# Attention and mixture of experts on one core: transposes as two 64-row halves, eight blocks to two PSUM banks, with six buffers for q and k

## The chip, the cores and the metric

The kernel runs on one core of one Trainium2 chip. The metric is the device time in microseconds of one execution, the median over several runs.

## The reference, cut to what matters

```python
def _attn_ref(q, k, v):                       # each (8, 8, 576, 64): batch, heads, sequence, head dim
    chunk = 64                                # 9 chunks of 64 positions, each attends to itself alone
    scores = (1 / np.sqrt(D)) * np.matmul(q_c, k_c.transpose(0, 1, 2, 4, 3))
    scores = scores - np.max(scores, axis=-1, keepdims=True)
    attn = np.exp(scores)
    attn = attn / (np.sum(attn, axis=-1, keepdims=True) + 1e-09)
    return np.matmul(attn, v_c).reshape(B, H, S, D)

def _moe_ref(x, w_gate, w_local, w1, w2):     # x: (8, 576, 512), 8 experts, F = 1024
    # each token takes the expert of its largest logit, or the one of the token before it,
    # as a local gate says; p is the softmax of the logits
    h = np.maximum(x[b, s] @ w1[e], 0.0)
    out[b, s] = p[e] * (h @ w2[e])
```

All of it is float32.

## The kernel before, in words

The 4608 tokens are 18 attention tiles of 256 tokens (four chunks of 64; tiles 4 and 13 are "mixed", they gather the ninth chunks of four batches). A tile goes through these steps, each a list of small functions ("atoms"):

- `load_qk` and `load_v` (lines 137 and 153) issue the DMAs of q, k and v on SP's queue. q and k have three buffers each, v has three (`vbuf`, the first in the raw tiles of w2).
- `pair_heads` (line 166, token `pr` or `p0` to `p3`) copies q and k into `qr` and `kr`, so that two heads lie side by side: 8 blocks of 128 rows by 128 columns each.
- `qk_transposes` (line 203, token `tq`) turns them over on TensorE: 8 blocks of q, 8 of k. `trans4` (line 186) takes four blocks into one PSUM bank (tile `tr`, pool `ps_tr` with three banks) and then has the bank copied out to `qT` or `kT`.
- `scores` (line 220, token `s`): 64 small matmuls 64x64 on the four quadrants of the array, then the largest of each row (`top`), the subtraction (`down`) and the exponential (`exp`).
- `p_transposes` (line 258, `tp`): 8 blocks of the probabilities, copied out to `pT`.
- `values` (line 267, `va`): two groups of 32 small matmuls, with `norm` behind each, into `xs`.
- `x_transposes` (line 304, `tx`): 8 blocks of `xs`, copied out to `xT`.
- `router` (line 312, `ra`): the logits (`lg`, 8 matmuls with 32 stationary columns each), two transposes, and the DMA of `xs` with its logits to `x_d` in DRAM.

In the trace TensorE's transposes all have line 192 and ScalarE's copies line 182, so they are told apart by their tiles. A transpose takes its block as the stationary operand and the identity as the moving one.

The order of the work on TensorE, VectorE, ScalarE and GpSimd is written out by hand in strings of tokens (`PAR`, line 47; `play`, line 523, walks through them): `"start"` brings in tiles 0 to 2, `"steady"` is one iteration of the loop on line 866 (i from 1 to 15, in which tile i+1 has its scores, tile i its probabilities turned, tile i-1 its values, tile i-2 its `xs` turned and routed, tile i+2 its q and k turned, tile i+3 paired, and q, k of tile i+5 and v of tile i+2 are loaded), and `"drain"` ends the attention and interleaves it with the routing and the first expert tiles. From i = 10 on, "hooks" (`h0` to `h3`) put the routing of the first half of the tokens between the tokens of the iteration, mostly on VectorE. From i = 8 to 15 each iteration also splits half a w1 tile. Loads are issued by SP in the order of the program and wait there for their buffer.

After the drain come the expert layers (lines 961 to 1222), which the change doesn't touch. Their w2 tiles `w2h` and `w2l` are first written in the drain (`w2_split`, line 882).

Of the kernel before, what the change touches and what calls it, by code (L numbers as in the profile page):

```python
# [8 lines left out]
F32 = mybir.dt.float32  # L9
F32R = mybir.dt.float32r  # L10
# [10 lines left out]
B, H, S, D = 8, 8, 576, 64  # L21
E, F = 8, 1024
C = H * D
N = B * S
P = 128
# [4 lines left out]
HT = P // 2  # L30
# [15 lines left out]

PAR = {
    "start": (
        "p0*4 t0a*4 t0a t0b*4 t0b t0c*4 t0c t0d*4 t0d p1*4 q3 t1a*4 t1a s0*8 t1b*4 t1b s0*2 t1c*4 t1c "
        "q4 t1d*4 t1d p2*4 s0*4 s1*8 t2a*4 t2a t2b*4 t2b s1*2 o0*4 o0 o0*4 o0 s1 t2c*4 t2c t2d*4 t2d s1*3 q5 v2 p3*4 io "  # L50
    ),
    "drain": (
# [13 lines left out]
    "t0": "VAVA",  # L66
    "t1": "AAAA",
    "t2": "AVAA",
    "steady": "lq va*4 va s*8 s h0 tx*8 tq*8 s h1 va*4 lv ra*2 va h2 tq*8 ra*2 tp*8 s pr*4 h3 ",
    "hooks": [43, 43, 45, 46, 47, 48, 49, 49, 51, 51, 52, 53, 54, 55, 55, 56, 57, 58, 59, 61, 61, 62],  # L70
}

# [2 lines left out]
def tile_attention_then_moe(ctx: ExitStack, tc, q, k, v, wg, wl, w1, w2, out):  # L75
    nc = tc.nc

    cpool = ctx.enter_context(tc.tile_pool(name="cpool", bufs=1))
    wpool = ctx.enter_context(tc.tile_pool(name="wpool", bufs=1))
# [7 lines left out]
    ident = cpool.tile([P, P], F32, name="ident")  # L87
# [2 lines left out]

    w1h = [wpool.tile([P, F], F32R, name=f"w1h{c}") for c in range(4)]
    w1l = [wpool.tile([P, F], F32R, name=f"w1l{c}") for c in range(4)]
    w2h = [wpool.tile([P, 2, C], F32R, name=f"w2h{c}") for c in range(4)]
    w2l = [wpool.tile([P, 2, C], F32R, name=f"w2l{c}") for c in range(4)]
    raw1 = [wpool.tile([P, F], F32, name=f"raw1_{c}") for c in range(4)]
    raw2 = [wpool.tile([P, 2, C], F32, name=f"raw2_{c}") for c in range(4)]

# [3 lines left out]
    def load_w2(e, c):  # L101
        nc.sync.dma_start(raw2[c], w2[e, 256 * c:256 * c + 256, :].rearrange("(f p) d -> p f d", p=P))
# [16 lines left out]
    ps_o = ctx.enter_context(tc.tile_pool(name="ps_o", bufs=1, space=PSUM))  # L119
    ps_l = ctx.enter_context(tc.tile_pool(name="ps_l", bufs=1, space=PSUM))  # L120

    vbuf = [[raw2[c].rearrange("p f (h d) -> p (f h) d", d=2 * D) for c in (2, 3)]]
    for i in range(2):
        vt = pa1.tile([P, VS], F32, name=f"v{i}")[:, 0:2 * H * DW].rearrange("p (c h d) -> p c h d", c=2, d=DW)
        vbuf.append([vt[:, c] for c in range(2)])

    def place(i):
        ph, j = divmod(i, 9)
# [5 lines left out]
    def mixed_rows(i):  # L134
        return i % 9 == LEFT

    def load_qk(i):
        qt = pe2.tile([P, 8 * 2 * D], F32, name="qt", tag="qt", bufs=3)
        kt = pe2.tile([P, 8 * 2 * D], F32, name="kt", tag="kt", bufs=3)
# [12 lines left out]

    def load_v(i):
        vt = vbuf[i % 3]
# [25 lines left out]
    def evac(eng, dst, src):  # L180
        if eng is nc.scalar:
            eng.copy(dst, src)
        else:
            eng.tensor_copy(dst, src)

    def trans4(src_of, evacs, fine=False):
        box = {}

        def one(n):
            if n == 0:  # L190
                box["ps"] = ps_tr.tile([P, 4, P], F32, name="tr")
            nc.tensor.transpose(box["ps"][:, n], src_of(n), ident)
            if n == 3 and not fine:
                for m in range(len(evacs)):
                    out(m)

        def out(m):
            eng, dst, sl = evacs[m]
            evac(eng, dst, sl(box["ps"]))

        return [lambda n=n: one(n) for n in range(4)] + [lambda m=m: out(m) for m in range(len(evacs)) if fine]

    def qk_transposes(i, hd, qT, kT, engs=None):
        atoms = []
        fine, engs = engs is not None, engs or QK_ENG
        for n, t in enumerate((qT, kT)):
            for x in range(2):
                if mixed_rows(i):
                    src = hd[n].rearrange("p (r h) j d -> p r h (j d)", r=2)[:, x]
                    dst = t.rearrange("a h (c p r) -> a r h c p", c=4, r=2)[:, x]  # L210
                    how = lambda ps: ps.rearrange("a h (p c) -> a h c p", c=4)
                else:
                    src = hd[n].rearrange("p (l x) j d -> p x l (j d)", x=2)[:, x]
                    dst = t.rearrange("a g (p l x) -> a x g p l", l=4, x=2)[:, x]
                    how = lambda ps: ps.rearrange("a l (p g) -> a g p l", g=4)
                atoms += trans4(lambda m, src=src: src[:, m], [(engs[2 * n + x], dst, how)], fine)
        return atoms


# [36 lines left out]
                      lambda: down(1), lambda: exp(4, 8)]  # L256

    def p_transposes(pr, pT, fine=False):
        atoms = []
        for g in range(2):  # L260
            atoms += trans4(
                lambda n, g=g: pr[:, 4 * g + n].rearrange("p c k -> p (c k)"),
                [(nc.scalar, pT[:, 4 * g:4 * g + 4], lambda ps: ps)], fine)
        return atoms


    def values(pT, vt, xs, fine=False):
        box = {}

        def group(j, h):  # L270
            if h == 0:
                box["o"] = ps_o.tile([P, 2, 512], F32, name="o")
            o = box["o"]
            for cp in range(2):
                for cc in range(2):
                    nc.tensor.matmul(
                        o[64 * cp:64 * cp + 64, cc, DV * h:DV * h + D + 1],
                        pT[64 * cc:64 * cc + 64, 4 * j + h, 64 * cp:64 * cp + 64],
                        vt[cp][64 * cc:64 * cc + 64, 4 * j + h, 0:D + 1],
                        start=True, stop=True,  # L280
                    )
# [14 lines left out]

        out = []
        for j in range(2):
            out += [lambda j=j, h=h: group(j, h) for h in range(4)]
            if fine:  # L300
                out.append(lambda j=j: norm(j))
        return out

    def x_transposes(xs, xT, fine=False):
        atoms = []
        for cc in range(2):
            atoms += trans4(
                lambda n, cc=cc: xs[:, cc, P * n:P * n + P],
                [(nc.scalar, xT[:, :, P * cc:P * cc + P], lambda ps: ps)], fine)
        return atoms  # L310

    def router(i, xT, xs, fine=False):
        lg = ps_l.tile([P, 2, 256], F32, name="lg")
# [174 lines left out]
    qk, hd, vts, qkT, prs, pTs, xss, xTs = ({} for _ in range(8))  # L488
# [11 lines left out]
        return scores(*qkT.pop(i), prs[i], fine)  # L500

    def a_tp(i, fine=False):
        pTs[i] = pa2.tile([P, H, P], F32, name="pT")
        return p_transposes(prs.pop(i), pTs[i], fine)

    rows = []
# [85 lines left out]
    with tc.manual_schedule(engines=MAN | {ET.Pool}):  # L592
# [10 lines left out]
        def tq(i, g):  # L603
# [283 lines left out]

    for c in range(2):
        load_w2(0, c)
    n = NS - 1  # L890
    sa = a_sa(n, True)
    run(sa[0:8])
# [351 lines left out]
```

## Time and profile before

| | |
|---|---|
| median of 3 runs | 650.43 us (645.71 to 650.65) |
| the profiled execution | 652.38 us |
| its span in the profile | 650.5 us, 1.9 us of that time lie around it |
| TensorE matmuls, weight loads | 94%, 79% of the span |
| VectorE, ScalarE, GpSimd | 58%, 39%, 23% |
| granted TensorE clock, mean | 0.991 of full |

A span is read from the first instruction to the last on the slowest core. PE is TensorE's matmul row, PEld its weight loads, DVE VectorE, ACT ScalarE, POOL GpSimd, SP SyncE. A matmul's record covers its whole way through the array, so consecutive records overlap: what one costs in a stream is the step from start to start. An instruction of matrix multiplication in float32 shows as two matmuls in scores, values and logits, a transpose as one.

### The profile page before, as it was taken

What the parts mean: (1) busy time and instruction counts of PE and PEld (TensorE: products, weight loads), DVE (VectorE), ACT (ScalarE), POOL (GpSimd) and SP (SyncE); (2) the same over time, 40 slices, a digit from 0 to 9 for tenths busy, and PEclk for the clock granted to TensorE, in tenths of its full rate; (3) what the DMA queues carried; (4) which work ended last, traced back from release to release, by engine and by line L of the source; (5) the groups of instructions that cost most, each with busy time, mean ns of one, the idle gap of its engine ahead of it and who ended that gap; (6) DMA issues with size and microseconds to landing.
All of it is one profiled execution on the core that took longest, in us unless ns stands there. A gap on an engine that the chain in (4) does not pass through costs nothing. (4 is left out here: it accounts for less than half of the span.)

```text
span 650.5 us, 17406 instructions
## 1 busy us (share of the span) xinstructions
PE 613.0 (94%) x5904; PEld 516.4 (79%) x5904; DVE 377.2 (58%) x983; ACT 256.5 (39%) x469; POOL 147.5 (23%) x217
## 2 busy tenths in 40 slices
PE   5889998999999999999999999999998999999995
PEld 4677777776778788788998996789887998788883
DVE  2666677986785667575334555753468533377231
ACT  4666675774421162532112343422454311343120
POOL 3623343570050302021021021031021222011101
PEclk9999998999999999999999999999998999999998
DMA  8799989998540155155021164442075511054201
GB/s 258 207 266 285 267 250 320 292 267 295 164 148 19 52 165 181 31 179 182 20 69 53 54 209 129 147 176 69 20 261 199 189 53 55 32 181 142 74 21 37
DMA packets 78360, 97.89 MB, mean 150 GB/s; under 512 B 42672, under 2 KB 46768, under 8 KB 78192
## 3 DMA queue, kind: packets, MB, share of 16 engines
q1 hardware_dynamic: 71744, 75.30, 37.1%
q0 software_dynamic: 6160, 19.99, 9.3%
q8 instruction: 86, 1.41, 0.9%
q14 instruction: 82, 0.67, 0.3%
q10 hardware_dynamic: 288, 0.52, 0.2%
HBM read 76.62 MB, written 19.69 MB: 148 GB/s over the span
## 5 line engine op out<-in xcount | busy, mean ns | idle before, releaser
L801 POOL DMA_INDIRECT out<-ysb,sidx x38 | 40.9, 1076 | 364.3 <-DVEq L997 163.3
L740 PE MATMUL y<-w2h,hq 128*128 128x512 f32 x368 | 119.8, 396 | 1.1 <-ACTq L1019 1.0
L1032 PEld LDWEIGHTS tr<-xp,w1h 128*128 128x128 f32 x704 | 87.8, 192 | 4.0 <-ACT w2h L981 1.1
L1032 PE MATMUL tr<-xp,w1h 128*128 128x256 f32 x704 | 90.2, 284 | 0.7 <-ACTq L997 0.4
L740 PEld LDWEIGHTS y<-w2h,hq 128*128 128x128 f32 x368 | 69.6, 189 | 16.7 <-issue 2.1
L740 PE MATMUL y<-w2l,hq 128*128 128x512 f32 x184 | 72.5, 394 | 2.6 <-DVE w2l L987 1.5
L1040 ACT ACTIVATE hq<-tr 128x256 fp32r<-128x256 f32 x68 | 25.3, 384 | 107.1 <-PE tr L1032 70.7
L740 PE MATMUL y<-w2h,hp 128*128 128x512 f32 x192 | 63.1, 396 | 0.4 <-ACT hp L687 0.3
L719 PE MATMUL h<-w1h,xp 128*128 128x512 f32 x208 | 60.8, 398 | 0.0
L1041 DVE SCALAR_TENSOR_TENSOR hq<-tr,hq 128x256 fp32r<-128x256 f32 x68 | 28.1, 423 | 38.1 <-ACT hq L1040 38.0
L1032 PE MATMUL tr<-xp,w1l 128*128 128x256 f32 x352 | 47.6, 283 | 0.0
L1032 PEld LDWEIGHTS tr<-xp,w1l 128*128 128x128 f32 x352 | 44.6, 192 | 0.0
L719 PEld LDWEIGHTS h<-w1h,xp 128*128 128x128 f32 x208 | 37.9, 189 | 7.6 <-ACTq L997 0.4
L740 PEld LDWEIGHTS y<-w2l,hq 128*128 128x128 f32 x184 | 34.9, 190 | 10.4 <-DVE w2l L987 2.4
L691 POOL DMA_INDIRECT xg<-x_d,gidx x36 | 38.3, 1063 | 19.6 <-issue 12.5
L740 PEld LDWEIGHTS y<-w2h,hp 128*128 128x128 f32 x192 | 36.0, 188 | 8.2 <-DVE hp L688 0.6
L786 ACT ACTIVATE hsb<-h 128x512 f32<-128x512 f32 x26 | 14.1, 596 | 65.8 <-PE h L719 56.4
L1061 DVE TENSOR_SCALAR ysb<-y,ppr 128x512 f32<-128x512 f32 x32 | 24.0, 750 | 26.9 <-PE y L740 23.8
L987 DVE TENSOR_TENSOR w1l<-raw,w1h 128x1024 fp32r<-128x1024 f32 x28 | 32.4, 1220 | 12.1 <-ACT w1h L981 10.6
L740 PE MATMUL y<-w2l,hp 128*128 128x512 f32 x96 | 37.6, 392 | 0.5 <-DVE w2l L987 0.5
L987 DVE TENSOR_TENSOR w2l<-raw,w2h 128x1024 fp32r<-128x1024 f32 x28 | 32.8, 1221 | 5.2 <-ACT w2h L981 3.2
L981 ACT CAST w2h<-raw 128x1024 fp32r<-128x1024 f32 x28 | 28.1, 1047 | 14.8 <-PE y L740 6.2
(229 smaller groups left out, 1062.1 us busy)
## 6 DMA issues: line engine op xcount, KB each, us to landing
raw<-in_moe_w SPq DMA_DIRECT2D x72, 512.0 KB, 5.1
x_d<-xs SPq DMA_DIRECT2D x16, 528.0 KB, 6.1
qt<-in_q SPq DMA_DIRECT2D x32, 256.0 KB, 5.0
kt<-in_k SPq DMA_DIRECT2D x30, 256.0 KB, 5.0
v<-in_v SPq DMA_DIRECT2D x20, 256.0 KB, 5.3
raw<-in_v SPq DMA_DIRECT2D x12, 256.0 KB, 5.2
x_d<-xs SPq DMA_DIRECT2D x4, 264.0 KB, 4.9
qt<-in_q SPq DMA_DIRECT2D x8, 128.0 KB, 3.8
```

Source lines behind the costliest of these rows:

```text
L691: nc.gpsimd.indirect_dma_start(out=dst, out_offset=None, in_=src, in_offset=bass.IndirectOffsetOnAxis(ap=gidx[t].bitcast(U32), axis=0))
L719: nc.tensor.matmul(hs[:, j], xs[a][:, c], W1[w][c][:, 512 * j:512 * j + 512], start=(c == 0 and n == 0), stop=(c == 3 and n == 2))
L740: nc.tensor.matmul(y, h_of(t, f // 4)[a][:, f % 4], W2[w][c][:, f % 2, :], start=(f == 0 and n == 0), stop=(f == 7 and n == 2))
L786: nc.scalar.activation(hsb[:, 512 * j:512 * j + 512], hs[:, j], AF.Relu)
L801: nc.gpsimd.indirect_dma_start(out=out, out_offset=bass.IndirectOffsetOnAxis(ap=sidx[t].bitcast(U32), axis=0), in_=ysb, in_offset=None, bo ...
L981: nc.scalar.copy(hi[c], raw[c])
L987: V.tensor_tensor(lo[c], raw[c], hi[c].bitcast(F32), ALU.subtract)
L1032: nc.tensor.matmul(hb[:, 256 * n:256 * n + 256], W1[w][c][:, P * (f + n):P * (f + n) + P], XP[:, x, c].rearrange("p s t -> p (s t)"), star ...
L1040: nc.scalar.activation(hi, ps, AF.Relu)
L1041: V.scalar_tensor_tensor(lo, ps, 0.0, hi.bitcast(F32), ALU.max, ALU.subtract)
L1061: V.tensor_scalar(ysb, y, pr, None, ALU.mult)
```

## The change

`trans8` takes the place of `trans4`. It turns each 128x128 block by two transposes: rows 0 to 63 of the block with the upper left quarter of the identity into columns of one PSUM bank, rows 64 to 127 with the lower right quarter into another bank. Eight blocks fill the two banks (8 times 64 columns each), and one copy empties each bank. The number of copies, and the elements of each, stay as they were. A group takes two of the three `tr` banks at once. `pT` gets the layout `[P, 2, H, 64]`, and `values` reads it so.

The buffers for q and k become six: three own ones and three in the tiles of w2 (`lent`); v gets four: two own ones, one in w2's tiles, one in the raw tiles of w2. The start issues the loads of tiles 3, 4 and 5 and of v 2 first; the steady iteration issues `lv` directly behind `lq`, scores stand ahead of the first values, and the tokens `tx`, `va`, `tq`, `ra` change places.

```diff
     "start": (
-        "p0*4 t0a*4 t0a t0b*4 t0b t0c*4 t0c t0d*4 t0d p1*4 q3 t1a*4 t1a s0*8 t1b*4 t1b s0*2 t1c*4 t1c "
-        "q4 t1d*4 t1d p2*4 s0*4 s1*8 t2a*4 t2a t2b*4 t2b s1*2 o0*4 o0 o0*4 o0 s1 t2c*4 t2c t2d*4 t2d s1*3 q5 v2 p3*4 io "
+        "q3 v2 q4 q5 p0*4 t0a*5 t0b*5 t0c*5 t0d*5 p1*4 t1a*5 t1b*3 s0*8 t1b*2 s0*2 t1c*5 t1d*5 "
+        "p2*4 s0*4 s1*8 t2a*5 t2b*5 s1*2 o0*10 s1 t2c*5 t2d*5 s1*3 p3*4 io "
     ),
...
-    "steady": "lq va*4 va s*8 s h0 tx*8 tq*8 s h1 va*4 lv ra*2 va h2 tq*8 ra*2 tp*8 s pr*4 h3 ",
+    "steady": "lq lv s*8 s h0 tx*8 s va*4 va tq*8 ra*2 h1 tq*8 va*4 va ra*2 h2 tp*8 s pr*4 h3 ",
...
-    vbuf = [[raw2[c].rearrange("p f (h d) -> p (f h) d", d=2 * D) for c in (2, 3)]]
+    qkbuf = [[pe2.tile([P, 8 * 2 * D], F32, name=f"{nm}{n}", bufs=1) for nm in ("qt", "kt")] for n in range(3)]
+    qkbuf += lent[0:3]
+    vbuf = []
...
+    vbuf.append([t.rearrange("p (h d) -> p h d", d=2 * D) for t in lent[3]])
+    vbuf.append([raw2[c].rearrange("p f (h d) -> p (f h) d", d=2 * D) for c in (2, 3)])
...
-    def trans4(src_of, evacs, fine=False):
-        box = {}
+    def trans8(src_of, evacs, fine=False, seq=range(8)):
+        ps = []
 
         def one(n):
-            if n == 0:
-                box["ps"] = ps_tr.tile([P, 4, P], F32, name="tr")
-            nc.tensor.transpose(box["ps"][:, n], src_of(n), ident)
-            if n == 3 and not fine:
-                for m in range(len(evacs)):
+            if n == seq[0]:
+                ps.extend(ps_tr.tile([P, 8, HT], F32, name="tr") for _ in range(2))
+            for r in range(2):
+                half = slice(HT * r, HT * r + HT)
+                nc.tensor.transpose(ps[r][:, n], src_of(n)[half], ident[half, half])
+            if n == seq[-1] and not fine:
+                for m in range(2):
                     out(m)
...
-                        pT[64 * cc:64 * cc + 64, 4 * j + h, 64 * cp:64 * cp + 64],
+                        pT[64 * cc:64 * cc + 64, cp, 4 * j + h],
...
-        pTs[i] = pa2.tile([P, H, P], F32, name="pT")
+        pTs[i] = pa2.tile([P, 2, H, HT], F32, name="pT")
```

The string `"drain"` stays as it is: a list of transposes had 4 blocks, a copy, 4 blocks, a copy, and has 8 blocks and two copies now, so its tokens fall on other atoms.

## Rows read from the trace of the kernel before

**Rows 1.** The page: TensorE's busy time, and the DMA share in 40 slices.

```profile
PE 613.0 (94%) x5904; PEld 516.4 (79%) x5904; DVE 377.2 (58%) x983; ACT 256.5 (39%) x469; POOL 147.5 (23%) x217
...
DMA  8799989998540155155021164442075511054201
```

**Rows 2.** Windows: busy time by engine, granted clock, DMA share and rate.

```profile
core 0: us, PE busy (x) PEld busy (x) DVE busy (x) ACT busy (x) POOL busy (x), PEclk, DMA share, GB/s
...
27.11:37.08 9.97, 7.47 (x187) 6.00 (x180) 5.16 (x13) 6.23 (x10) 6.68 (x27) 1.00 0.86 246
37.08:90.11 53.03, 49.74 (x1200) 41.50 (x1196) 36.27 (x91) 36.53 (x64) 17.88 (x30) 1.00 0.94 276
75.33:82.56 7.23, 6.98 (x183) 5.87 (x178) 5.16 (x13) 5.21 (x10) 2.37 (x4) 1.00 0.98 265
90.11:140.27 50.16, 45.46 (x1033) 37.63 (x1025) 42.56 (x135) 34.02 (x60) 26.31 (x37) 0.97 0.98 282
...
98.78:103.45 4.67, 4.36 (x104) 4.11 (x105) 2.74 (x7) 0.54 (x2) 1.27 (x1) 0.63 1.00 330
```

**Rows 3.** Timeline of TensorE, one steady iteration: start, length, instructions, idle before.

```profile
75.33 1.11 PE L227 MATMUL sc<-kT,qT 64*64 64x64 f32 x64
76.37 1.09 PE L192 MATMUL tr<-ident,xs 128*128 128x128 f32 x8
77.30 1.18 PE L192 MATMUL tr<-ident,qr 128*128 128x128 f32 x8
78.41 0.70 PE L276 MATMUL o<-v,pT 64*64 64x65 f32 x32
79.04 0.64 PE L318 MATMUL lg<-xT,wg 128*32 128x256 f32 x8
79.61 1.10 PE L192 MATMUL tr<-ident,kr 128*128 128x128 f32 x8
80.54 0.38 PE L327 MATMUL lg<-ident,lT 128*128 128x128 f32 x2
80.76 1.04 PE L192 MATMUL tr<-ident,pr 128*128 128x128 f32 x8
82.05 0.70 PE L276 MATMUL o<-v,pT 64*64 64x65 f32 x32 [0.25 <-ACT pT L182]
82.56 1.11 PE L227 MATMUL sc<-kT,qT 64*64 64x64 f32 x64
```

**Rows 4.** Groups by form, TensorE and weight loads, 27.11 to 140.27 us.

```profile
L227 PE MATMUL sc<-kT,qT 64*64 64x64 f32 x896 | 17.2, 225 | 1.1 <-issue 1.1
L192 PE MATMUL tr<-ident,pr 128*128 128x128 f32 x112 | 14.8, 275 | 0.2
L318 PE MATMUL lg<-xT,wg 128*32 128x256 f32 x112 | 8.9, 391 | 0.3 <-issue 0.3
...
L227 PEld LDWEIGHTS sc<-kT,qT 64*64 64x64 f32 x896 | 15.7, 141 | 1.3 <-issue 1.3
L192 PEld LDWEIGHTS tr<-ident,pr 128*128 128x128 f32 x112 | 12.5, 141 | 0.9 <-ACT kT L182 0.7
L318 PEld LDWEIGHTS lg<-xT,wg 128*32 128x32 f32 x112 | 2.3, 108 | 1.2 <-issue 0.2
```

**Rows 5.** Groups by form, ScalarE, 75.33 to 82.56 us.

```profile
L182 ACT COPY xT<-tr 128x512 f32<-128x512 f32 x2 | 1.1, 590 | 0.9 <-PE tr L192 0.9
```

**Rows 6.** Timeline of TensorE: two waits, and the work behind one.

```profile
36.61 0.62 PE L276 MATMUL o<-v,pT 64*64 64x65 f32 x26 [1.54 <-DMA v<-in_v]
...
98.78 0.33 PE L276 MATMUL o<-v,pT 64*64 64x65 f32 x4 [2.12 <-DVE ab L384]
...
101.74 1.87 PE L192 MATMUL tr<-ident,xs 128*128 128x128 f32 x8
```

**Rows 7.** Windows, as rows 2: the 20 us with the highest rate.

```profile
100.00:120.00 20.00, 18.89 (x430) 15.82 (x423) 15.97 (x46) 12.94 (x23) 7.36 (x11) 0.92 1.03 317
```

**Rows 8.** Timeline of SP's queue: the issue of v's third tile.

```profile
29.89 1.22 SPq L159 DMA_DIRECT2D v<-in_v  x2
```

More of the change, by code (lines that the diff above doesn't have):

```diff
@@ L92, in tile_attention_then_moe @@
     w1l = [wpool.tile([P, F], F32R, name=f"w1l{c}") for c in range(4)]
-    w2h = [wpool.tile([P, 2, C], F32R, name=f"w2h{c}") for c in range(4)]
-    w2l = [wpool.tile([P, 2, C], F32R, name=f"w2l{c}") for c in range(4)]
+    w2h, w2l = [], []
+    lent = [[wpool.tile([P, 8 * 2 * D], F32, name=f"lent{nm}{c}", tag=f"w2{nm}{c}", bufs=1) for nm in "hl"] for c in range(4)]
     raw1 = [wpool.tile([P, F], F32, name=f"raw1_{c}") for c in range(4)]
@@ L137, in load_qk @@
     def load_qk(i):
-        qt = pe2.tile([P, 8 * 2 * D], F32, name="qt", tag="qt", bufs=3)
-        kt = pe2.tile([P, 8 * 2 * D], F32, name="kt", tag="kt", bufs=3)
+        qt, kt = qkbuf[i % len(qkbuf)]
         for m, (b, s0, n) in enumerate(place(i)[1]):
@@ L153, in load_v @@
     def load_v(i):
-        vt = vbuf[i % 3]
+        vt = vbuf[i % len(vbuf)]
         t0 = 0
@@ L184, in evac @@
             eng.tensor_copy(dst, src)
-    def trans4(src_of, evacs, fine=False):
-        box = {}
+    def trans8(src_of, evacs, fine=False, seq=range(8)):
+        ps = []
         def one(n):
-            if n == 0:
-                box["ps"] = ps_tr.tile([P, 4, P], F32, name="tr")
-            nc.tensor.transpose(box["ps"][:, n], src_of(n), ident)
-            if n == 3 and not fine:
-                for m in range(len(evacs)):
+            if n == seq[0]:
[5 more added lines that the diff above has]
+                for m in range(2):
                     out(m)
         def out(m):
-            eng, dst, sl = evacs[m]
-            evac(eng, dst, sl(box["ps"]))
-        return [lambda n=n: one(n) for n in range(4)] + [lambda m=m: out(m) for m in range(len(evacs)) if fine]
+            eng, dst, how = evacs[m]
+            evac(eng, dst, how(ps[m]))
+        return [lambda n=n: one(n) for n in seq] + [lambda m=m: out(m) for m in range(2) if fine]
     def qk_transposes(i, hd, qT, kT, engs=None):
@@ L206, in qk_transposes @@
         for n, t in enumerate((qT, kT)):
-            for x in range(2):
+            evacs = []
+            for r in range(2):
                 if mixed_rows(i):
-                    src = hd[n].rearrange("p (r h) j d -> p r h (j d)", r=2)[:, x]
-                    dst = t.rearrange("a h (c p r) -> a r h c p", c=4, r=2)[:, x]
-                    how = lambda ps: ps.rearrange("a h (p c) -> a h c p", c=4)
-                else:
[L213 to L216, printed above, removed]
+                    dst = t.rearrange("a h (c p r) -> a h c p r", c=4, r=2)[:, :, :, 16 * r:16 * r + 16]
+                    how = lambda ps: ps.rearrange("a (r h) (p c) -> a h c p r", r=2, c=4)
+                else:
+                    dst = t[:, :, P * r:P * r + P].rearrange("a g (p m) -> a g p m", m=8)
+                    how = lambda ps: ps.rearrange("a m (p g) -> a g p m", g=4)
+                evacs.append((engs[2 * n + r], dst, how))
+            atoms += trans8(lambda m, n=n: hd[n][:, m].rearrange("p j d -> p (j d)"), evacs, fine,
+                             range(8) if mixed_rows(i) else [m for x in range(2) for m in range(x, 8, 2)])
         return atoms
@@ L258, in p_transposes @@
     def p_transposes(pr, pT, fine=False):
[L259 to L264, printed above, removed]
+        return trans8(lambda n: pr[:, n].rearrange("p c k -> p (c k)"),
+                      [(nc.scalar, pT[:, r], lambda ps: ps) for r in range(2)], fine)
     def values(pT, vt, xs, fine=False):
@@ L304, in x_transposes @@
     def x_transposes(xs, xT, fine=False):
[L305 to L310, printed above, removed]
+        xv = xT.rearrange("a n (c p q) -> a p c n q", c=2, p=2)
+        return trans8(lambda n: xs[:, n // 4, P * (n % 4):P * (n % 4) + P],
+                      [(nc.scalar, xv[:, r], lambda ps: ps.rearrange("a (c n) q -> a c n q", c=2)) for r in range(2)], fine)
     def router(i, xT, xs, fine=False):
@@ L889, in tile_attention_then_moe @@
         load_w2(0, c)
+    for nm, ts in (("h", w2h), ("l", w2l)):
+        ts.extend(wpool.tile([P, 2, C], F32R, name=f"w2{nm}{c}", tag=f"w2{nm}{c}", bufs=1) for c in range(4))
     n = NS - 1
```

## The prediction

> **What bounds the kernel now.** The page first: TensorE is busy 94% of the span, and the DMA engines are at 0.8 to 0.99 in the first ten slices and mostly under 0.5 later [rows 1]. Those ten slices are the attention, and the change touches nothing behind the drain, so only the attention and the drain, up to about 180 us, can move; what they lose the end loses, since TensorE is full from there on.
>
> The windows next [rows 2]. I cut the attention at the starts of the scores: tile 3's at 27.11 us, tile 17's at 140.27. One iteration (27.11 to 37.08) took 9.97 us, the next seven 53.03 (7.58 each), the last six, with the routing hooks, 50.16 (8.36 each). In the seven TensorE is busy 94% and the DMA share is 0.94 at 276 GB/s; in the six VectorE is busy 42.56 of 50.16 us and the DMA share is 0.98 at 282 GB/s. So two or three resources are near full at once, and that decides how much of a TensorE saving can be kept.
>
> The timeline of one undisturbed iteration of 7.23 us [rows 3] gives TensorE's prices, from start to start. Scores: 1.04 us for 64, 16 ns each. Eight transposes: 0.93 us (76.37 to 77.30), 116 ns a block. Values: 0.51 us where scores follow (82.05), 0.63 where the logits follow (78.41). Probabilities: 1.29 us, of which 0.25 is a shown wait for the copy of `pT`. All four groups of transposes take 0.93 + 1.11 + 0.93 + 1.29 = 4.26 us.
>
> **The change part by part.**
>
> *Half the columns per transpose.* A matmul's record is 225 ns for 64 moving columns, 275 for 128, 391 for 256 [rows 4]: 64 columns fewer are 50 ns fewer. Each block is now two transposes of 64 columns, one on each row half. That the halves run beside each other is borne out by the scores: four quadrants, both halves among them, step by 16 ns while one record is 225. I take the block at 116 - 50 = 66 ns. Bounds: below, two steps of the scores, 33 ns; above, no gain at all, 116 ns, and worse if the halves follow each other (the last rival). The load is the doubtful part: two loads of 128 columns a block. A load's record is 108 ns for 32 columns and 141 for 128 [rows 4], so 96 columns add only 33 ns, and it should hide behind the 50 ns of the matmul; I stay at 66. 32 blocks an iteration give 32 x 50 = 1.6 us.
>
> *More changes of the array's shape.* Transposes were 128x128 and are 64x128 now, and the values stand apart between the groups. In today's order the shape changes five times an iteration (scores to `xs`, `qr` to values, values to logits, logits to `kr`, `pr` to values). In the new order it changes nine times. The rows price a change: values 0.63 - 0.51 = 0.12 us, `qr` to values 1.11 - 0.93 = 0.18 us, scores to transposes about nothing (1.04 us is 64 steps of 16 ns) [rows 3]. Four more cost between 0 and 0.72 us; I take 0.6, since three of the four stand next to values or logits.
> [...]
>
> *Waits.* With scores ahead of the values, the copy of `pT` lies behind 1.04 us of scores, so the 0.25 us wait goes. A new one comes: a group needs two of three banks, so its second half waits for the first copy of the group before. That copy takes 0.59 us [rows 5] and starts some 0.15 us behind the last transpose (an estimate from the 275 ns record against the 116 ns step), so the bank is free 0.75 us after a group. Between the groups lie values 0.63, logits 0.57, values and two transposes 0.73 to 0.85, scores 1.04 [rows 3]: two of four are short, by about 0.1 to 0.2 us. Behind the waiting transpose the whole of TensorE's queue stands. I take 0.25 us; bounds 0 and 0.59 x 4 = 2.4. The two waits cancel.
>
> TensorE's iteration: 7.23 - 1.6 + 0.6 - 0.25 + 0.25 = 6.2 us. ScalarE (5.21) and VectorE (5.16) fit under it [rows 2]; the number of copies is as before, their shapes hardly change.
>
> *DMA.* The bytes per tile stay. The 53.03 us stretch moves 14.6 MB (276 GB/s), the six iterations 14.1 MB. How far the rate can go: 317 GB/s over the best 20 us, at a share of 1.03 [rows 7], and 330 over 4.67 us [rows 2]. With buffers that are never waited for, SP can keep its queue full; I take 305 GB/s, halfway between 282 and 330, for both. Then the seven iterations need 14.6 / 0.305 = 48.0 us, more than TensorE's 7 x 6.2 = 43.6: the DMA is what is late next. Saved: 53.0 - 48.0 = 5.0 us. The six need 14.1 / 0.305 = 46.4 us, above VectorE's 42.6, so 50.2 - 46.4 = 3.8 us. In these the shown wait of 2.12 us for a routing step (`ab`) may stay [rows 6].
>
> *Buffers and start.* The values of tile 2 waited 1.54 us for their v [rows 6]; SP had issued it at 29.89 us [rows 8], behind tiles 3 to 5. It stands directly behind tile 3 now. That wait goes, and what is late next is the DMA again (2.45 MB at 305 GB/s is 8.0 us): of 9.97 us I take off 2.0. Before 27.11 us some transposes are faster and others still wait for their loads: 1.0 off, bounds 0 and 3. The tiles lent from w2 cost nothing: their last users are q and k of tiles 15 to 17, paired before the loop ends, and v of tile 14, multiplied in its last iteration; w2 is split after it.
>
> *Drain.* 48 blocks at 50 ns are 2.4 us. The order string is the old one, groups hold two banks each there, and the expert work takes banks of the same pool: I give back more than half, and take 1.0 us off, bounds +2 and -2.4.
>
> Sum: -5.0 - 3.8 - 2.0 - 1.0 - 1.0 = -12.8 us. The profiled execution took 652.38 us, so 639.6; the median of the runs is 0.3% below that, 650.43, which gives 637.7. **638 us.**
>
> **The rivals.**
>
> *The DMA keeps up.* At 330 GB/s, or if part of the load was ahead by then, TensorE sets the pace: 7 x 6.3 = 44 us (-9), the six go to VectorE's 43 to 45 (-6), and with -2.5, -1 and -1 it is about 631 us. For it: 330 GB/s is shown. Against it: only for 4.67 us.
>
> *The DMA is at its end already.* A share of 0.94 and 0.98 leaves 3.2 and 1.0 us. With the 4 us elsewhere: 642 us, inside my range.
>
> *The transposes gain nothing.* The load takes the place of the matmul and a block stays at 116 ns. TensorE's iteration is then 7.23 + 0.6 = 7.8 us, 0.25 over today's 7.58 in the seven; over 13 iterations about +3 to +5, less 3 for the start and v: 651 us, no change.
> [...]
>
> *Slower: the halves follow each other.* If the two row halves are not loaded and run side by side, a half costs at least its 66 ns, a block 132: TensorE's iteration is 7.23 + 32 x 0.016 + 0.6 = 8.3 us, 0.8 over 7.58, times 13 is +10, drain and start +1 to +2: 662 us; with the loads uncovered as well (141 ns each, a block up to 280) it is +5 us an iteration and over 700. It decides from the point where a block costs over about 108 ns (7.58 us an iteration). Against it: the 16 ns step of the scores on both halves. [...]
>
> **How the numbers follow.** Forecast with its kin (631 to 644, the DMA at its end included): 0.60. DMA keeps up, under 631: 0.12. No gain from the transposes, 644 to 656: 0.18. Slower, over 657: 0.10. A measurement of this kernel tells about 1% from no change, 6.5 us: under 643.9 is faster. Nearly all of the first two and a little less of their edge is that, 0.71; same 0.19; slower 0.10. The likeliest case's own range is 631 to 644. For 8 in 10 I leave out half of the cases under 630 and those over 652: 627 to 652.
>
> **What would show it.** The step between blocks of `tr`: 66 ns if right, 116 or more if the load binds. The iteration between 45 and 90 us: 6.7 to 7.0 us, with TensorE waiting on DMA, or on POOL's copies that wait for it, and a DMA rate near 305 GB/s. Values to logits, and each change of shape, 0.12 to 0.18 us. No wait of values for `pT`, none for v at tile 2; instead waits of `tr` for copies of ScalarE, parts of a microsecond. The granted clock near 1.00 from 30 us on. The last scores (140.27 us now) at about 128. What would make it wrong: a DMA rate that stays at 276 to 282, blocks over 100 ns, or a clock that falls.

## The result, and the profile after

The changed kernel takes 655.98 us in the median of 20 runs (651.75 to 660.92), the kernel before, on the same chip, 648.48 us (20 runs, 644.48 to 652.07): a ratio of 1.0115, with a 95% interval of 1.0094 to 1.0137. It is slower, by about 1%; 638 us was forecast, and the range ended at 652. Its profiled execution has a span of 655.4 us, 4.9 us more than that of before; the medians are 7.5 us apart, so what follows accounts for 4.9 us of these.

The page of the changed kernel, TensorE's row as in [rows 1], with the instruction queue's row (packets, MB, share of 16 engines; 86 packets before):

```profile
PE 607.7 (93%) x6480; PEld 507.2 (77%) x6480; DVE 379.0 (58%) x983; ACT 254.5 (39%) x469; POOL 147.4 (22%) x219
...
q8 instruction: 90, 1.47, 0.9%
```

TensorE is busy 5.3 us less with 576 more matmuls, so the transposes did become cheaper. The time is lost between them.

I cut the attention at the starts of the scores, as in the prediction. Tile 3's start at 31.87 us (27.11 before), tile 4's at 38.38 (37.08), tile 11's at 94.70 (90.11), tile 17's at 145.03 (140.27), and the first matmul with w2 (`y`; those with w1 are interleaved in the drain) is at 177.58 (172.61). So the start lost 4.8 us; the iteration to tile 4 won 3.5 (6.51 for 9.97); the next seven lost 3.3 (56.3 for 53.0); the last six lost 0.2 (50.33 for 50.16), and the drain 0.2 (32.55 for 32.34). Together that is 5.0 us, the 4.9 of the span but for 0.1.

Windows of the changed kernel, columns as in [rows 2]: a stretch between the same times as there, the last of the seven iterations, undisturbed, and the one behind it; then the two slowest of the seven, and the parts of these two in which the clock was low:

```profile
37.08:90.11 53.03, 44.52 (x1369) 35.19 (x1358) 34.01 (x85) 33.97 (x60) 14.98 (x28) 0.94 0.98 285
87.87:94.70 6.83, 6.29 (x206) 5.06 (x202) 5.17 (x14) 5.66 (x10) 3.61 (x5) 1.00 0.82 215
94.70:101.53 6.83, 6.32 (x206) 5.09 (x202) 5.11 (x14) 5.66 (x10) 3.61 (x5) 1.00 1.03 337
69.03:78.09 9.06, 7.32 (x206) 5.65 (x202) 5.35 (x14) 5.25 (x9) 2.34 (x4) 0.81 0.98 272
78.09:87.87 9.78, 7.74 (x206) 5.92 (x203) 5.25 (x14) 5.14 (x9) 2.34 (x4) 0.83 0.91 277
73.03:76.44 3.41, 3.41 (x56) 2.26 (x48) 1.49 (x4) 1.84 (x4) 1.17 (x2) 0.50 1.06 261
83.27:86.68 3.41, 3.41 (x65) 2.37 (x65) 0.42 (x1) 1.70 (x4) 1.73 (x4) 0.50 0.86 252
```

In 37.08 to 90.11 TensorE is busy 44.5 us of 53 where it was 49.7 [rows 2]: it waits 8.5 us. An undisturbed iteration takes 6.83 us (7.23 before), but two of the seven take 9.06 and 9.78, at a granted clock of 0.81 and 0.83, where before the clock was 1.00 throughout the seven.

The timeline of TensorE over the undisturbed iteration, as [rows 3]:

```profile
87.87 1.16 PE L233 MATMUL sc<-kT,qT 64*64 64x64 f32 x64
88.96 0.71 PE L197 MATMUL tr<-ident,xs 64*128 64x64 f32 x16
89.61 0.69 PE L277 MATMUL o<-v,pT 64*64 64x65 f32 x32
90.23 0.27 PE L197 MATMUL tr<-ident,qr 64*128 64x64 f32 x1
91.05 0.70 PE L197 MATMUL tr<-ident,qr 64*128 64x64 f32 x15 [0.54 <-ACT xT L185]
91.68 0.64 PE L316 MATMUL lg<-xT,wg 128*32 128x256 f32 x8
92.25 0.89 PE L197 MATMUL tr<-ident,kr 64*128 64x64 f32 x16
93.07 0.69 PE L277 MATMUL o<-v,pT 64*64 64x65 f32 x32
93.70 0.44 PE L325 MATMUL lg<-ident,lT 128*128 128x128 f32 x2
94.07 0.71 PE L197 MATMUL tr<-ident,pr 64*128 64x64 f32 x16
94.70 1.16 PE L233 MATMUL sc<-kT,qT 64*64 64x64 f32 x64
```

Sixteen halves, which are eight blocks, step by 0.63 to 0.65 us (94.07 to 94.70, 88.96 to 89.61): 80 ns a block, the change of shape included, where a block took 116. Within a group the records of the blocks stand 63 ns apart in the median of the seven iterations, 109 in the kernel before, so the load does not hold a block at its old price. (`kr` takes 0.82 us, 92.25 to 93.07: its second block starts 0.18 us behind the first, a short wait that the view merges.)

What TensorE waited for in 37 to 90 us (line, releaser, us in total, times, longest), first the kernel before, then the changed one:

```profile
PE o L276 <- ACT pT L182: 1.9, 7, 0.3
PE sc L227 <- issue: 1.1, 2, 0.8
```

```profile
PE tr L197 <- issue: 4.7, 3, 2.0
PE o L277 <- issue: 2.7, 2, 1.6
PE sc L233 <- issue: 0.9, 2, 0.5
```

The wait for `pT` is gone, as forecast. In its place stand 8.3 us of "issue": TensorE waits, and no semaphore, copy or DMA of data releases it. That is the new wait, and the prediction does not name it.

Its places tell what it is. The timeline of the changed kernel's TensorE from one such wait to the next, and the starts of two more:

```profile
56.73 0.58 PE L277 MATMUL o<-v,pT 64*64 64x65 f32 x25 [1.64 <-issue]
57.24 0.71 PE L197 MATMUL tr<-ident,qr 64*128 64x64 f32 x16
57.88 0.64 PE L316 MATMUL lg<-xT,wg 128*32 128x256 f32 x8
58.45 0.94 PE L197 MATMUL tr<-ident,kr 64*128 64x64 f32 x16
59.32 0.69 PE L277 MATMUL o<-v,pT 64*64 64x65 f32 x32
59.95 0.44 PE L325 MATMUL lg<-ident,lT 128*128 128x128 f32 x2
60.31 0.71 PE L197 MATMUL tr<-ident,pr 64*128 64x64 f32 x16
60.96 0.45 PE L233 MATMUL sc<-kT,qT 64*64 64x64 f32 x12
61.83 1.03 PE L233 MATMUL sc<-kT,qT 64*64 64x64 f32 x52 [0.42 <-issue]
...
66.82 0.65 PE L197 MATMUL tr<-ident,kr 64*128 64x64 f32 x14 [0.94 <-issue]
...
83.04 0.87 PE L197 MATMUL tr<-ident,qr 64*128 64x64 f32 x13 [2.01 <-issue]
83.83 1.08 PE L316 MATMUL lg<-xT,wg 128*32 128x256 f32 x8
84.84 1.12 PE L197 MATMUL tr<-ident,kr 64*128 64x64 f32 x16
```

The waits fall in the middle of a group: between two values, two scores, two transposes of one kind, where nothing in the program asks for a wait. The counts are regular: 25+16+8+16+32+2+16+12 = 127 matmuls from the first to the second, 52+16+32+16+8+2 = 126 from there to the third. With a weight load to each that is 254 and 252 instructions. Seven of these waits lie between 38 and 95 us (1.04, 0.48, 1.64, 0.42, 0.94, 1.74 and 2.01 us, 8.3 together), always 126 to 128 matmuls apart or twice that. In the DMA view of 80.0 to 83.2 us the instruction queue moves one packet of 0.02 MB (packets, MB, share), and TensorE waits from 81.03 until 83.04:

```profile
q8 instruction: 1, 0.02, 1.8%
```

The trace has the times of each packet: all seven waits end 1.1 to 1.5 us behind the end of a packet of this queue (this one ends at 81.53), and the three of the kernel before from 37 to 150 us 1.3 to 1.6 us behind one. The 576 matmuls more and their loads, 1152 instructions, go with four packets more. I read these figures so: TensorE's instructions arrive in pieces of some 254 (252 to 256 from one wait to the next, or twice that), each a packet of 0.02 MB on the DMA engines, and a piece can come too late.

An iteration had 170 matmuls and has 202 now, and takes less time: by these counts a piece that lasted 127/170 x 7.23 = 5.4 us lasts 127/202 x 6.43 = 4.0 us, 6.43 us being the iteration of a run below that has no loads. Behind two of the long waits, of 1.74 and 2.01 us, comes a second loss. From 83.04 the eight logits step by 1.01 us, not 0.57, and 16 halves by 1.05, not 0.64. The windows above have the granted clock to it: 0.50 from 73.03 to 76.44 and from 83.27 to 86.68 us. Behind the wait of 1.64 us, at 56.73, it stayed at 1.00. Against the undisturbed iteration, its own wait for `xT` left aside, the work behind 71.92 and behind 83.04 us is 1.2 to 1.3 us longer.

So the seven iterations come out as 7 x 6.43 (the run without loads) + 8.3 + 2 x 1.2 = 55.7 us; measured were 56.3.

The start, same view and kernel:

```profile
10.41 1.11 PE L197 MATMUL tr<-ident,qr 64*128 64x64 f32 x15 [0.67 <-ACT kT L185]
11.45 1.98 PE L233 MATMUL sc<-kT,qT 64*64 64x64 f32 x64
```

One half of a group runs, then TensorE waits 0.45 to 0.67 us until the group before has been copied out of a bank; that occurs six times by 28.70 us. And the pace is low until 31.87 us (16 halves 1.05 us, scores 1.98 to 2.36), where before it was full from the first scores on (1.31 at 10.87, 1.16 at 14.88). The windows print a granted clock of 1.00 for these 32 us, but the trace has no record of the clock ahead of 32.07 us (11.23 in the kernel before), so that figure says nothing here.

### The profile page after: what moved, and what is told of

It is laid out like the page before. It is cut to its first block, busy times and chain, and to the rows that moved or that the text cites. A ratio compares the mean times of both kernels' runs of the same rounds, so it can differ in the third digit from the quotient of the medians.

```text
span 655.4 us, 18524 instructions
## 1 busy us (share of the span) xinstructions
PE 607.7 (93%) x6480; PEld 507.2 (77%) x6480; DVE 379.0 (58%) x983; ACT 254.5 (39%) x469; POOL 147.4 (22%) x219
```

## Experiments

A number behind "Measured" is the ratio to the kernel before, measured beside it, with its 95% interval; stretches and waits are read from one profiled execution of each run.

**The first four: which part of the change costs.** *Whole blocks in the start alone:*

```diff
-        return qk_transposes(i, hd.pop(i), *qkT[i], engs)
+        return (qk_full if engs is not None else qk_transposes)(i, hd.pop(i), *qkT[i], engs)
-        return p_transposes(prs.pop(i), pTs[i], fine)
+        return (p_full if i == 0 else p_transposes)(prs.pop(i), pTs[i], fine)
```

(`qk_full` and `p_full` are the transposes of the kernel before, written to the new tiles.)

> The changed kernel, but the start (q and k of tiles 0 to 2, probabilities of tile 0) transposes whole 128-row blocks again, four to a bank. Start theory: the third scores stood at 31.87 us instead of 27.11 because a group holds two of three banks, waits 0.6 us for a copy each time, and the array with its gaps runs at half pace until 32 us; then the third scores come back to 27 or 28 us and the time falls by 4 to 5 us against the changed kernel, to 2.5 to 3.5 us above before. Rival (the loads set the start, or the loop's DMA takes back what is won): under 1.5 us, the time stays at +6 to +7.5 us.

Measured: 1.0099 [1.0066, 1.0133]. Tile 3's scores start at 27.5 us, so the halves do cost the start 4.4 of its 4.8 us. But the total hardly moves: issue waits are 9.5 us in 20 to 150 us, and tile 17's scores start at 141.3 us, 3.7 ahead of the changed kernel and 1.0 behind the kernel before. The whole executions show less of the gain than the profiled ones; why, stays open. The loop here is that of the changed kernel, yet the seven iterations took 53.3 us and the last six 53.8, not 56.3 and 50.3 (54.8 and 51.2 in the run with twelve matmuls of the identity, below). So where in the loop the late pieces fall changes between executions, and a split of one profile by stages is good to some 3 us.

*Halves alone, with the buffers and orders of before:*

```diff
-            nc.tensor.transpose(box["ps"][:, n], src_of(n), ident)
+            for r in range(2):
+                half = slice(HT * r, HT * r + HT)
+                nc.tensor.transpose(ps[r][:, n], src_of(n)[half], ident[half, half])
```

> The kernel before with the halved transposes alone: old buffers, old order of the loads, old orders of the start and of the iteration. If the buffers and the new order are what costs the time in the last iterations and in TensorE's issue waits (8.6 us of them from 27 to 143 us in the changed kernel, 1.4 before), this one keeps the loss of the start (about 4.5 us) and gains 5 us or more in the loop: -3 to +1 us against before. If the halves themselves bring the issue waits (more instructions): +3 to +6 us.

Measured: 1.0319 [1.0254, 1.0383], which I had not expected. The waits of TensorE in 20 to 150 us (line, releaser, total, times, longest):

```profile
PE o L274 <- ACT pT L182: 10.5, 28, 0.6
PE tr L194 <- ACT xT L182: 9.6, 14, 1.0
```

In the old order two groups stand back to back, and two banks out of three make the second one wait for the copies of the first, 0.6 to 0.7 us in most cases; and the values, which follow the probabilities directly there, wait for the copies of `pT`.

*Buffers and orders alone, with whole blocks:*

```diff
-                nc.tensor.transpose(ps[r][:, n], src_of(n)[half], ident[half, half])
+            nc.tensor.transpose(box["ps"][:, n], src_of(n), ident)
```

> The change without the halves: six buffers, new orders, whole-block transposes four to a bank. If the halves cause the start's loss and the issue waits: the start is as before or 1 us better, the wait of tile 2 for its v is gone, -2 to -5 us against before, and issue waits of TensorE stay under 3 us. If the new order or the fuller DMA queue causes them: issue waits of 5 us or more and 0 to +5 us.

Measured: 1.0023 [0.9989, 1.0058], no difference, where 2 to 5 us less were expected. The issue waits are 2.6 us. The buffers and orders by themselves gain nothing that shows; the halves make the difference.

*Halves and buffers, with the old order of the iteration:*

```diff
-    "steady": "lq lv s*8 s h0 tx*8 s va*4 va tq*8 ra*2 h1 tq*8 va*4 va ra*2 h2 tp*8 s pr*4 h3 ",
+    "steady": "lq va*4 va s*8 s h0 tx*8 tq*8 s h1 va*4 lv ra*2 va h2 tq*8 ra*2 tp*8 s pr*4 h3 ",
```

> The changed kernel with the old order of the steady iteration (halves, buffers and start as changed). Order theory: the last seven iterations (57.2 us changed, 50.1 before) come back by 4 to 6 us, since the norm of the first values goes ahead of the routing hooks on VectorE again, total +1 to +3.5 us against before. If the order is not the cause: the stretch stays at 55 to 58 us and the total at +6 to +8 us.

Measured: 1.0245 [1.0214, 1.0276]. Slower than the changed kernel, so the new order isn't what costs: the halves need it. (The expectation set seven iterations of the changed kernel, 57.2 us, against six of before, 50.1; the same six take 50.3 there and 58.4 here.)

**Is it the supply of instructions?** Two theories are left for the loop: late instructions, or loads of data that take the DMA engines. *No loads of v from tile 4 on* (those values are then computed from old rows, and the routing differs, so the total isn't comparable):

```diff
         vt = vbuf[i % len(vbuf)]
+        if i >= len(vbuf):
+            return vt
```

> The changed kernel without the loads of v from tile 4 on (the old rows are used again): a quarter of the loop's bytes is left out. TensorE's issue waits come every 254 of its instructions or a multiple, so the theory is that a block of its instructions has to be fetched over the same DMA engines as the data, and that the halves (some 400 TensorE instructions an iteration instead of 340, in less time) use a block up in 4.2 us, before the next has come. Then with fewer data bytes the fetch is quicker: issue waits of TensorE under 3 us (8.6 in the changed kernel), tiles 4 to 11 in 46 to 48 us (56.3), total 7 us or more below the changed kernel. If only the count of instructions decides, the issue waits stay at 7 us or more, and the time falls by under 3 us.

Measured: ratio 1.1097 [1.106, 1.1134], issue waits 11.1 us. A miss, and it tells nothing: SP ran ahead with the other loads, at 337 GB/s in 40 to 60 us and 351 in 80 to 100, so the engines were as full as before where it mattered (a DMA share of 0.99 and 1.01).

*Half as many score matmuls, each over twice the columns* (half of the scores are computed against the neighbouring keys, so the routing and the total differ):

```diff
-                        sc[64 * cp:64 * cp + 64, j, h, cc, :],
...
-                        kT[64 * j:64 * j + 64, h, 64 * ch:64 * ch + 64],
+                    sc[64 * cp:64 * cp + 64, j, h].rearrange("p c k -> p (c k)"),
...
+                    kT[64 * j:64 * j + 64, h, 64 * ch:64 * ch + 128],
```

> The changed kernel with half as many matmuls in the scores, each with twice the columns (half of the score blocks are not computed, others are products of different chunks): the same columns through the array, 64 TensorE instructions fewer an iteration, as many as before the change. Fetch theory: issue waits fall from 8.6 us to under 4 us and the time by 3 us or more. If the fuller DMA queues alone delay the fetches: the waits stay at 7 us or more and the time within 2 us of the changed kernel.

The total, not comparable, is 1.0324 of before. The stretch from tile 4's scores to tile 11's, 39.1 to 87.2 us, columns as in [rows 2]:

```profile
39.10:87.20 48.10, 44.97 (x1193) 34.80 (x1190) 36.24 (x92) 36.74 (x64) 17.69 (x30) 1.00 0.97 286
```

48.1 us instead of 56.3, with a DMA share of 0.97 and a rate of 286 GB/s, as in the changed kernel; the clock stays at 1.00, and the issue waits are 2.1 us in all. The 32 scores take TensorE 1.04 us (45.54 to 46.58 us), the 64 took 1.09. So the scores take TensorE as long, in 64 instructions fewer an iteration, just as many as the halves had added.

*The converse, in the kernel before: eight logit matmuls cut into 32 of a quarter of the columns*, 48 instructions more an iteration:

```diff
-                nc.tensor.matmul(lg[32 * c:32 * c + 32, 0], wg9[:, c], xT[:, c], start=True, stop=True)
+            for z in range(0, 256, 64):
+                for c in range(4):
+                    nc.tensor.matmul(lg[32 * c:32 * c + 32, 0, z:z + 64], wg9[:, c], xT[:, c, z:z + 64], start=True, stop=True)
```

> The kernel before, with the logits of a tile computed in four pieces of 64 columns instead of one of 256: nothing else, 48 TensorE instructions more an iteration, the same columns. Fetch theory: the iteration's 388 instructions make a block last 4.8 us, so issue waits rise from 1.4 us to 4 us or more, and the time by 3 to 8 us. If the count of instructions is not what matters: issue waits under 2.5 us, the time within 2 us (the pieces add under 0.1 us an iteration).

Measured: 1.0083 [1.005, 1.0117]. The logits take no longer (62.35 to 62.94 us, 0.59 for 0.57). Waits of TensorE in 20 to 150 us:

```profile
PE lg L319 <- issue: 2.5, 2, 1.6
PE o L276 <- issue: 2.5, 2, 1.3
PE sc L227 <- issue: 1.9, 3, 1.3
```

With one on the routing's transposes, 7.5 us of issue waits, for 1.4 in the kernel before: the loss comes without the change, from more instructions alone.

*No loads of q and k from tile 6 and of v from tile 4 on* (later tiles compute on old rows; a single execution, total not comparable):

```diff
         qt, kt = qkbuf[i % len(qkbuf)]
+        if i >= len(qkbuf):
+            return qt, kt
         vt = vbuf[i % len(vbuf)]
+        if i >= len(vbuf):
+            return vt
```

> The changed kernel without the loads of q and k from tile 6 on and of v from tile 4 on (the old rows are used again, so only the time of the attention loop can be compared): from about 40 us on the DMA engines carry xs to DRAM and w1 alone. If the fetches of TensorE's instructions are late because the data fill the DMA engines: issue waits of TensorE between 45 and 100 us fall to 1 us or less (6.3 us between 45 and 90 in the changed kernel) and iterations to 6.5 to 6.9 us. If a fetch takes its time by itself: 4 us or more of issue waits stay.

One time, 709.08 us. Windows over three iterations behind the last load:

```profile
58.90:78.20 19.30, 19.06 (x610) 15.16 (x609) 15.47 (x40) 15.42 (x27) 7.02 (x12) 1.00 0.27 88
```

19.3 us for three iterations, 6.43 each. In the timeline issue waits stand at 39.07 us (1.80) and 46.39 (1.33), while the loads run, and the waits of 47 to 100 us hold no "issue" at all, with all the halves' instructions in place. So in these runs pieces came late where two things met: they were used up in some 4 us (an estimate from the counts; under 5 with the split logits), and data filled the DMA engines (a share of 0.97 in the seven, 0.27 here). Not each piece did: the changed kernel's iteration from 94.70 us has both, 6.83 us at a DMA share of 1.03, and no such wait. What decides it from piece to piece, these runs don't show. (Between 45 and 90 us the changed kernel has 7.2 us of issue waits, not the 6.3 of the expectation.)

**The start and the buffers.** *Twelve matmuls of the identity ahead of the first transposes*, against the low pace of the start:

```diff
+        wps = ps_l.tile([P, 512], F32, name="wps", tag="lg")
+        for _ in range(12):
+            nc.tensor.matmul(wps[:, 0:P], ident, ident, start=True, stop=True)
```

> The changed kernel with 12 extra matmuls of the identity on TensorE ahead of the first transposes, in the time in which it waits for the first loads. Clock theory of the start: the transposes from 6.8 us on run at full pace (16 halves in 0.7 us instead of 1.1) and the third scores come at 27 to 29 us instead of 31.9; total 1 to 4 us less than the changed kernel. If the bank waits alone cost the start: the third scores stay at 30.5 us or later.

Measured: 1.0126 [1.0089, 1.0163], no gain. The timeline of its start:

```profile
10.10 0.70 PE L197 MATMUL tr<-ident,qr 64*128 64x64 f32 x15 [0.67 <-ACT kT L185]
10.74 1.89 PE L233 MATMUL sc<-kT,qT 64*64 64x64 f32 x64
```

The first groups run at full pace, and from 10.74 us on the scores are at half pace again, behind two waits for banks (0.65 us at 8.72, 0.67 at 10.10). Here the trace does record the clock, at 0.50 until 31.38 us:

```profile
10.90:31.38 20.48, 16.73 (x380) 14.74 (x380) 10.08 (x19) 9.34 (x18) 10.98 (x43) 0.50 0.89 242
```

The waits come first and the low pace after them; how the 4.8 us divide between the two stays open.

*Three buffers and the old places of the loads, with halves and the new order of the iteration:*

```diff
-        qt, kt = qkbuf[i % len(qkbuf)]
+        qt = pe2.tile([P, 8 * 2 * D], F32, name="qt", tag="qt", bufs=3)
+        kt = pe2.tile([P, 8 * 2 * D], F32, name="kt", tag="kt", bufs=3)
```

> The halves and the new order of the iteration with the old three buffers for q, k and v (v loaded behind the second values again). If the six buffers' fuller queue is what delays the instruction fetches: issue waits of 4 us or less and 3 us or more below the changed kernel. If the halves' instructions cause them whatever the buffers: 7 us or more of issue waits and a total within 3 us of the changed kernel, or above it by the wait of tile 2 for its v.

Measured: 1.0156 [1.0115, 1.0197], issue waits 10.7 us: loads that run further ahead are not the cause.

**Fewer halves.** With whole blocks in the start and the drain, *halves for xs and the probabilities of the loop only*, and *for q and k of the loop only* (cut; the start of the second as in the first run):

```diff
-        return qk_transposes(i, hd.pop(i), *qkT[i], engs)
+        return qk_full(i, hd.pop(i), *qkT[i], engs)
```

> Halves only for xs and the probabilities in the loop (32 more TensorE instructions an iteration instead of 64); q and k, the start and the drain in whole blocks, buffers and orders as changed. Fetch theory: 372 instructions at about 6.9 us an iteration, a block of 254 lasts 4.7 us, the start as before the change: issue waits 2 to 5 us, total -3 to +1 us against before. If a block must last over 5 us to be safe whatever the mix: issue waits above 6 us and +2 us or more.

```diff
-        return p_transposes(prs.pop(i), pTs[i], fine)
+        return p_full(prs.pop(i), pTs[i], fine)
-        return x_transposes(xss[i], xTs[i], fine)
+        return x_full(xss[i], xTs[i], fine)
```

> Halves only for q and k in the loop, whole blocks for xs, probabilities, the start and the drain. The count of instructions is that of the kernel with halves for xs and probabilities, so the same issue waits, 2 to 5 us, and -3 to +1 us against before; more bank waits than there, since q and k follow each other with only the logits between.

Measured: 1.0104 [1.0053, 1.0154] with issue waits of 8.5 us, where 2 to 5 were expected and the rival said above 6, and 1.0034 [1.0009, 1.0059] with 4.0. Of either sum 1.6 us are four short waits in the last scores, some 0.75 us and 2 to 4 matmuls apart: late pieces of some 254 do not explain these. The second run gains for a while: tile 4 to tile 11 in 50.0 us, tile 11's scores at 84.8 us, 5.3 ahead of the kernel before. Its last six iterations then take 54.4 us, and the gain is gone. TensorE waits there 3.1 us for VectorE's `xs`, 2.4 us for loads of v and 0.3 us of "issue", and the granted clock is 0.94.

*To see where: q and k of tiles 3 to 12 only, whole blocks after that; and beside it all four groups of the same iterations.*

```diff
-        return (qk_full if engs is not None else qk_transposes)(i, hd.pop(i), *qkT[i], engs)
+        return (qk_full if engs is not None or i > 12 else qk_transposes)(i, hd.pop(i), *qkT[i], engs)
```

> Halves only for q and k of tiles 3 to 12; whole blocks in the start, the last six iterations and the drain; buffers and orders of the changed kernel. Theory (the last six iterations pay for the halves as well, through late instructions): the scores of tile 11 start at 85 us as with halves for q and k throughout, the six that follow take 49 to 50 us as with whole blocks, the first expert matmul comes at 166 to 167 us, and the ratio to the kernel before is 0.990 to 0.994. Rival (the last six wait for VectorE's routing steps and for loads whatever the transposes cost): the six take 53 to 55 us, the scores of tile 17 stay at 139 to 140, ratio 1.000 to 1.005.

```diff
+        return (p_full if fine or i > 10 else p_transposes)(prs.pop(i), pTs[i], fine)
...
+        return (x_full if fine or i > 8 else x_transposes)(xss[i], xTs[i], fine)
```

> As the run beside it, but the halves also for xs and the probabilities of the same iterations. Theory: 64 more instructions an iteration come late here, so the issue waits up to tile 11 are 5 us or more and tile 11's scores start at 87 to 89 us, 2 to 4 us later than with q and k alone; then the six as whole blocks, ratio 0.995 to 1.000. Rival: the number of instructions does not matter in itself, and tile 11's scores start at 84 us or before, since 16 more halved blocks an iteration save TensorE time; ratio as in the run beside it or lower.

Measured: 1.0081 [1.0049, 1.0113] and 1.0147 [1.0116, 1.0178]. Both lie above what was expected. In the first the scores of tile 11 start at 86.7 us and the six iterations take 51.0: neither the 49 to 50 of the theory nor the 53 to 55 of the rival. (The program is that of the run with q and k throughout up to there, and that had 84.8: the same work varies by 1.9 us.) Tile 17's scores start at 137.7 us, 2.6 ahead of before, and the drain, all in whole blocks, takes 35.3 us to the first matmul with w2 (172.97) where 32.34 had done. Its timeline:

```profile
139.68 0.33 PE L283 MATMUL sc<-kT,qT 64*64 64x64 f32 x4 [0.42 <-issue]
140.44 1.19 PE L283 MATMUL sc<-kT,qT 64*64 64x64 f32 x33 [0.42 <-issue]
142.01 1.33 PE L232 MATMUL tr<-ident,pr 128*128 128x128 f32 x5 [0.39 <-ACT pr L302]
```

The short issue waits in the last scores again, and behind them five whole blocks in 1.33 us (0.76 at 142.03 us in the kernel before); the granted clock of the drain is 0.90, where it was 1.00. The second run has 10.1 us of issue waits and reaches tile 11's scores at 91.4 us, 4.7 later than with q and k alone: the second half of the added instructions costs more than its blocks save. None of these versions is faster than the kernel before.

## Why the prediction was wrong, step by step

- **Half the columns per transpose: right.** A block steps by 63 ns, for 66 forecast, and by 80 with its share of the shape change, for which 0.6 us an iteration had been taken besides. 7.23 us became 6.43 in the run without loads; 6.2 was forecast.
- **The seven iterations, -5.0 us: this is the step that failed.** Measured +3.3 (53.3 to 54.8 us in the two runs with the same loop, so +0.3 to +1.8 there). The sum priced the array, the copies and the bytes of data, but not the instructions themselves: 64 more an iteration, in a shorter iteration. They cost 8.3 us of issue waits and, behind these, about 2.4 us at a granted clock of 0.50, where the sum had nothing. "The DMA is what is late next" was right about the resource and wrong about what it was late with: SP's loads kept up (TensorE's waits on data in the seven are nil), instructions did not. The rate was over 305 GB/s for a time (311 from 45 to 69 us, so the rival of a DMA at its end falls) and 280 over the seven, and more was not needed: the wide scores ran the seven in 48.1 us, the 48.0 of the forecast, at 286. The signs were in the trace of before: 1.1 us of "issue" on the scores in [rows 4], which I passed over.
- **The last six, -3.8 us: wrong, +0.2.** The sum let the DMA alone set the pace there, at 305 GB/s; the rate was 274. TensorE is busy 3.4 us less (42.07 for 45.46 us) and waits 3.6 us more. Its two largest waits from 94.70 to 145.03 us are:

```profile
PE o L277 <- DVE xs L291: 3.7, 3, 2.1
PE tr L197 <- ACT xT L185: 2.1, 4, 0.6
```

Before, these places had 2.1 us (for `ab` [rows 6]) and 0.8. Two VectorE routing steps took longer: two `qeq` 1.21 us, 0.35 before, one `qv` 1.28, 0.26 to 0.30 before. But they don't decide it: whole blocks with the new buffers and orders had them as long (1.21 and 1.33) and ran the six in 49.5 us, and halves for q and k alone had them short (0.33 and 0.27) and took 54.4. No version with all its loads ran these six in less than 49 us; why, stays open.

- **Tile 3 to 4, -2.0 us: right in kind, -3.5.** The wait for v is gone. Part of it the late start gave: with whole blocks in the start, TensorE waits here for GpSimd's `qr`, 1.3 to 2.0 us in four runs, 0.3 and 0.6 in two, and not at all in the changed kernel.
- **The start, -1.0 us (bounds 0 and 3): wrong, +4.8.** I priced the wait for banks in the loop, where values or logits lie between two groups (0.25 us an iteration; 0.5 were measured at `xT` in the undisturbed one), and not in the start, where groups follow each other and the whole copy is waited for, six times, with the array at the low pace besides (16 halves in 1.05 us, 0.64 later).
- **The drain, -1.0 us: +0.2**, inside its bounds.
- **The rivals.** "The halves follow each other" is refuted by the 80 ns, "the transposes gain nothing" by the same; that the median of 655.98 us lies just inside the range given to the latter (644 to 656) is chance. The clock, named last among what would make the forecast wrong, did fall: to 0.50 for 3.41 us twice in the seven, at 1.2 to 1.3 us each, behind waits of 1.74 and 2.01 us for instructions, which the sum did not have. What makes it fall is not shown: behind 1.64 us it stayed at 1.00.
- **A reading.** The first ten slices have the DMA engines at 0.7 to 0.99, not 0.8 [rows 1]; nothing hangs on it.

Shown by runs: the halves cost it and not buffers or order (the second to fourth run), the instructions' number by itself (wide scores, split logits), and that it takes DMA engines busy with data (no loads). Open: what binds the last six, the share of clock and banks in the start, and which pieces come late.

## What to carry to other kernels

Halving an operand to use the array better doubles the instructions: count them against the time. Where TensorE used up some 254 in about 4 us while loads filled the DMA engines (a share of 0.97 here; at 0.27 nothing was late, and what lies between no run shows), it waited for its own program at times, 8.3 us over seven iterations, and the granted clock was 0.50 behind two of the long waits (1.74 and 2.01 us) and 1.00 behind a third (1.64). An "issue" row in the waits, in the middle of a group and regularly spaced, was the sign; try it by cutting an unrelated matmul into pieces. A saving on one engine should be followed to the end of the kernel: here a run that led by 5.3 us at tile 11 was 1.9 us behind at the first matmul with w2 (174.48 us).

## What the runs showed of the hardware

- TensorE's "issue" waits in the seven iterations came every 252 to 256 of its instructions (matmuls and loads), or twice that, and each ended 1.1 to 1.5 us behind a packet of 0.02 MB in the instruction queue; 1152 instructions more went with four packets more. Read as pieces that come late: pieces lasting 5.4 us (an estimate from the counts) by 1.1 us in all at a DMA share of 0.94, pieces lasting 4.0 us by 8.3 at 0.97; at 0.27 there was no wait.
- Two transposes of 64 rows on the two row halves take 80 ns a block (116 for 128 rows), 63 (109) within a group, with two loads of 128 columns that the records give 144 ns each in the mean.
- In the start the windows print a granted clock of 1.00 while 16 halves take 1.05 us against 0.64 later: the trace's records of the clock begin at 32.07 us only. In the run with twelve matmuls ahead they reach into the start, and the granted clock of 10.90 to 31.38 us is 0.50: there the durations tell the pace, and a figure without a record doesn't.
